# A state-space scan and a gated feed-forward on one core: block 0's scan as a pipeline over all PSUM banks, masked copies of C on ScalarE, the float64 conversion in two stages over three engines

## The chip, the core and the metric

The kernel runs on one core of a Trainium2 chip. A core has five engines that run their own queues in order and wait for each other through semaphores: TensorE (PE, matrix multiplies; its weight loads are listed apart as PEld), VectorE (DVE), ScalarE (ACT), GpSimd (POOL) and SyncE (SP, which here only issues DMAs). SBUF is the working memory of 128 partitions; PSUM holds what TensorE writes, in 8 banks of 128 x 512 float32. GpSimd has no access to PSUM in this kernel. The metric is the device time of one execution in microseconds, the median of several runs.

## The reference

Four sequences of 768 positions with 8 heads go through a linear recurrence (a state of 16 x 32 for each head), the heads are put side by side to rows of 256, and those rows go through a feed-forward with a cosine gate. Cut to what is computed:

```python
log_a = np.log(np.clip(a, 1e-06, 1.0))
for c in range(nc):                       # a, B, C, x of one chunk of 32 positions
    cum = np.cumsum(la, axis=-1)
    L = np.exp(cum[:, :, :, None] - cum[:, :, None, :]) * causal
    M = np.einsum('bhin,bhjn->bhij', Cc, Bc) * L
    y[:, :, sl] = (np.einsum('bhij,bhjd->bhid', M, xc)
                   + np.einsum('bhin,bhnd->bhid', Cc, state) * np.exp(cum)[:, :, :, None])
    state = decay_full * state + np.sum(Bx, axis=2)
x = y.transpose(0, 2, 1, 3).reshape(B * S, H * D)      # 3072 x 256
h = x @ w_in                                           # 256 -> 2048
out = ((h * np.cos(h)) @ w_out).astype(np.float32)     # 2048 -> 256
```

Here x, a, B and C are float32, and `w_in` and `w_out` are float64: the kernel reads each weight as two 32-bit words and makes a float32 of them by arithmetic on the bits.

## The kernel before, in words

The sequence is cut into NC = 6 blocks of 128 positions. A block c has a scan for each of the four sequences ("batches", b) and a feed-forward over its 512 rows in NF = 16 steps f of 128 hidden columns.

The scan of one batch is written in four functions. `decays` makes `lam`, the decay matrix of all 8 heads, as a running product on VectorE (L231; in block 0 on PSUM tiles `a_ps` that TensorE fills with broadcast rows of `cut`, L242 and L244; in later blocks on rows `arow` that DMAs broadcast). `turn` transposes B, the decay-scaled C (`sc`) and C on TensorE (`tp`, L254), copies two of them to `bcT` on ScalarE (L256) and makes `cT`, four masked copies of C for the heads, on VectorE (L259). `intra` multiplies them (`g`, L270) and applies `lam` on VectorE (`m`, L273). `finish` multiplies with x (`y`, L286), copies the result to `yT` on ScalarE (L291), and makes the next state (`s_ps` on TensorE L295, `state` on VectorE L299, in later blocks two GpSimd operations). `prep` scales B and C of a block on GpSimd (`sc`, L220) with `dec`, the exponentials of summed logarithms that TensorE and ScalarE make at the start (L197 to L208).

A feed-forward step is `first` (two multiplies into `hp`, L314; `w` and `k` on ScalarE in block 0, `turns` on VectorE), `gate` one step later (`cos` on ScalarE, `gT` on VectorE) and `second` three steps later (four multiplies into `o`, L340). `hp` has three PSUM banks, so `hp` of step n needs `gT` of step n − 3. The scan's tiles, `a_ps` among them, share three more banks (tag "scan"), and `o` has the last two.

The weights come in 16 pieces of 128 x 512 elements, 8 of `w_in` and 8 of `w_out`, each good for two steps. `convert` takes one piece: ScalarE shifts the low word (`part`, L141), VectorE does four operations on the high word (`mag`: mask the sign L144, limit L146, shift L148, merge with sign and exponent L150), GpSimd adds the two (L154). The order of all work is written by hand: the program text is each engine's order. In it block 0's scan comes first, with three conversions ahead of it, batch after batch with `turn`, `intra`, `finish` in a row; then the 16 steps of block 0, each with one more conversion and a third of a batch of block 1's scan; then the same for later blocks without conversions. SP issues all loads but the first three pieces in the order of the text.

## Time and profile before

| | |
|---|---|
| median of 3 runs | 477.78 us (477.05 to 479.7) |
| the profiled execution, its own time | 476.28 us |
| its span on the core | 474.6 us |
| TensorE busy | 430.6 us (91%) |
| VectorE, ScalarE, GpSimd busy | 308.2, 153.6, 65.5 us |
| chain that ended last | PE 83%, DVE 13% of the span |

The page gives busy time of an engine over the whole span, a strip of 40 slices with the clock that the throttle granted to TensorE, the chain of work that ended last, and groups of instructions by line. A timeline gives single rows in order of time: start, length, engine, line, operation, tile written and tiles read, shape, count, and in brackets how long the engine had been idle and what ended that. A table of stretches gives each engine's busy time in a stretch, the granted clock and the DMA share. The end of a TensorE row is modelled, and rows of float32 matrix multiplies come two for one instruction.

### The profile page before, as it was taken

How to read it: one execution, taken by the hardware profiler on the slowest of the kernel's cores; microseconds unless marked ns; L12 is line 12 of the kernel's file. 1: busy time of each engine (PE TensorE's matmuls, PEld its weight loads, DVE VectorE, ACT ScalarE, POOL GpSimd, SP SyncE). 2: the span in 40 equal slices, each digit the busy share in tenths (PEclk: the TensorE clock that was granted, in tenths of full speed). 3: DMA queues.
4: the chain of work that ended last, by engine and by line, in shares of the span. 5: the costliest groups of instructions: out<-in, count | busy, mean ns of one | idle time of the engine just before them, and what ended most of it. 6: DMA issues, size and time to landing. Idle time of an engine off the chain costs nothing.

```text
span 474.6 us, 5058 instructions
## 1 busy us (share of the span) xinstructions
PE 430.6 (91%) x1896; PEld 274.5 (58%) x1896; DVE 308.2 (65%) x468; ACT 153.6 (32%) x285; POOL 65.5 (14%) x72
## 2 busy tenths in 40 slices
PE   5067757988999999999999999999999999999996
PEld 5044324644666666666666666666666656666665
DVE  3834599777666677657666758666667767455452
ACT  4000254523543223234232323332333322342331
POOL 2310054342250101120111020111200000000000
PEclk9657879988999999999999999999999999999999
DMA  9998049511091111371111752001101000010001
GB/s 184 274 148 251 0 134 141 81 44 46 2 133 45 44 46 44 60 74 45 46 45 46 84 50 88 27 19 44 46 0 44 1 1 1 0 46 0 0 1 46
DMA packets 102873, 28.84 MB, mean 61 GB/s; under 512 B 74816, under 2 KB 98752, under 8 KB 102848
## 3 DMA queue, kind: packets, MB, share of 16 engines
q1 hardware_dynamic: 102032, 26.94, 30.2%
q10 hardware_dynamic: 816, 1.57, 1.0%
q8 instruction: 15, 0.25, 0.2%
q14 instruction: 10, 0.08, 0.1%
HBM read 25.26 MB, written 3.24 MB: 60 GB/s over the span
## 4 chain that ended last, share of the span: by engine, by line
PE 83%; DVE 13%; issue 2%; ACT 1%; POOL 1%; POOLq 0%; ACTq 0%
PE hp L314 34%; PE o L340 32%; PE g L270 6%; PE y L286 3%; PE s_ps L295 3%; DVE lam L244 2%; PE y L282 2%; DVE mag L146 2%; DVE lam L231 2%; DVE mag L144 1%; PE tp L254 1%; DVE mag L148 1%; DVE cT L259 1%; PE a_ps L242 1%; DVE turns L325 1%
## 5 line engine op out<-in xcount | busy, mean ns | idle before, releaser
L314 PE MATMUL hp<-yT,w_in 128*128 128x512 f32 x384 | 189.9, 619 | 5.8 <-DVE gT L332 5.8
L340 PEld LDWEIGHTS o<-w_out,gT 128*128 128x128 f32 x768 | 146.4, 191 | 61.1 <-issue 46.1
L340 PE MATMUL o<-w_out,gT 128*128 128x256 f32 x768 | 180.9, 379 | 0.0
L318 ACT ACTIVATE w<-hp 128x512 f32<-128x512 f32 x96 | 57.4, 598 | 218.6 <-PE hp L314 218.6
L314 PEld LDWEIGHTS hp<-yT,w_in 128*128 128x128 f32 x384 | 71.8, 197 | 75.3 <-issue 66.0
L323 DVE TENSOR_SCALAR k<-w 128x512 f32<-128x512 f32 x80 | 36.6, 457 | 99.9 <-ACT w L318 99.9
L325 DVE SCALAR_TENSOR_TENSOR turns<-k,w 128x512 f32<-128x512 f32 x96 | 68.6, 715 | 16.6 <-ACT k L321 13.8
L332 DVE TENSOR_TENSOR gT<-hp,cos 128x512 f32<-128x512 f32 x96 | 65.6, 683 | 0.2 <-ACT cos L330 0.2
L330 ACT ACTIVATE cos<-turns 128x512 f32<-128x512 f32 x96 | 59.8, 622 | 2.5 <-DVE turns L325 2.5
L231 DVE TENSOR_TENSOR_SCAN lam<-arow,unit 128x1024 f32<-128x1024 f32 x20 | 45.6, 2281 | 0.0
L270 PE MATMUL g<-cT,bcT 64*128 64x512 f32 x96 | 29.2, 686 | 13.2 <-DVE cT L259 13.1
L305 POOL TENSOR_TENSOR state<-state,old 128x256 f32<-128x256 f32 x16 | 12.3, 766 | 186.7 <-DVE state L299 186.5
L273 DVE TENSOR_TENSOR m<-g,lam 128x512 f32<-128x512 f32 x48 | 30.7, 682 | 6.5 <-PE g L270 6.5
L291 ACT COPY yT<-y 128x256 f32<-128x256 f32 x24 | 9.0, 373 | 46.8 <-PE y L286 46.8
L299 DVE TENSOR_TENSOR state<-s_ps,own 128x256 f32<-128x256 f32 x20 | 8.5, 424 | 20.3 <-PE s_ps L295 20.3
L154 POOL TENSOR_TENSOR w_in<-mag,part 128x512 uint32<-128x512 uint32 x8 | 12.7, 1593 | 56.5 <-DVE mag L150 54.5
L286 PE MATMUL y<-m,xr 128*32 128x128 f32 x384 | 17.3, 294 | 3.4 <-DVE m L273 3.4
L270 PEld LDWEIGHTS g<-cT,bcT 64*128 64x128 f32 x96 | 7.4, 189 | 21.3 <-DVE cT L259 21.3
L154 POOL TENSOR_TENSOR w_out<-mag,part 128x512 uint32<-128x512 uint32 x8 | 14.5, 1809 | 33.8 <-DVE mag L150 31.7
L259 DVE TENSOR_TENSOR cT<-tp,slot 128x512 f32<-128x512 f32 x24 | 16.0, 668 | 4.0 <-ACT bcT L256 4.0
L256 ACT COPY bcT<-tp 128x256 f32<-128x256 f32 x24 | 8.9, 370 | 29.2 <-PE tp L254 29.2
L254 PE MATMUL tp<-ident,sc 128*128 128x128 f32 x24 | 6.7, 281 | 12.1 <-POOL sc L220 12.1
(52 smaller groups left out, 214.5 us busy)
## 6 DMA issues: line engine op xcount, KB each, us to landing
arow<-a_cut SPq DMA_DIRECT2D x20, 512.0 KB, 3.8
words<-in_moe_w_out_dram SPq DMA_DIRECT2D x8, 512.0 KB, 3.7
xr<-in_x_dram SPq DMA_DIRECT2D x6, 512.0 KB, 8.6
out_dram<-ob SPq DMA_DIRECT2D x12, 256.0 KB, 2.3
words<-in_moe_w_in_dram SPq DMA_DIRECT2D x5, 512.0 KB, 7.5
words<-in_moe_w_in_dram ACTq DMA_DIRECT2D x3, 512.0 KB, 6.5
bc<-in_B_dram SPq DMA_DIRECT2D x6, 256.0 KB, 6.6
bc<-in_C_dram SPq DMA_DIRECT2D x6, 256.0 KB, 9.1
```

The source lines that it names most:

```text
L154: G.tensor_tensor(out=dst.bitcast(U32), in0=bits.rearrange("p (k f) -> p k f", k=k), in1=part_.rearrange("p (k f) -> p k f", k=k), op=ALU.add)
L231: V.tensor_tensor_scan(out=l.rearrange("p h i -> p (h i)"), data0=arow.pop((c, b)).rearrange("p h i -> p (h i)"), data1=unit.rearrange("p ...
L270: PE.matmul(g[u], lhsT=bcT[r, 0], rhs=cT[r], start=True, stop=True)
L273: V.tensor_tensor(out=m[:, hs], in0=g[u], in1=l[:, hs], op=ALU.mult)
L286: PE.matmul(y[32 * q:32 * q + 32, t], lhsT=xr[:, b, h], rhs=m[:, h], start=(c == 0 and t == 0), stop=True, tile_position=(0, 32 * q), skip ...
L314: PE.matmul(hp[n], lhsT=w_in[:, k, f * P:(f + 1) * P], rhs=yT[c][:, k], start=(k == 0), stop=(k == KT - 1))
L318: ACT.activation(w, hp[n], AF.Copy, bias=0.25, scale=INV_2PI)
L323: V.tensor_scalar(out=k_, in0=w, scalar1=ROUND, scalar2=None, op0=ALU.add)
L325: V.scalar_tensor_tensor(out=turns[n], in0=k_, scalar=ROUND, in1=w, op0=ALU.subtract, op1=ALU.subtract)
L330: ACT.activation(cos, turns.pop(n), AF.Sin, scale=-TWO_PI)
L332: V.tensor_tensor(out=gT[n], in0=hp.pop(n), in1=cos, op=ALU.mult)
L340: PE.matmul(o[c][b // 2][:, b % 2], lhsT=g[:, b * P:(b + 1) * P], rhs=w_out[:, f], start=(f == 0 and b % 2 == 0), stop=(f == NF - 1), skip ...
```

## The change

Block 0's scan is written as a pipeline. `a_ps` is made by `spread_a`, ahead of everything on TensorE, for three of the four batches into banks of all three tags ("h" and "o" aren't in use yet), for the fourth when the first two banks are free. The logarithm's path moves into `whole`, behind them. `cut` is limited by GpSimd itself instead of being a copy of VectorE's result. `turn` for batch b + 1 or b + 2 stands ahead of `intra` for b, block 0 doesn't make the scaled C any more (its first state is zero), and the states of block 0 are made in `carry` after all four batches. `cT` is made by four ScalarE copies with a scale per partition, in all blocks; VectorE's operation goes. Conversion is split: `grade` (ScalarE takes the absolute value and shifts the low word, GpSimd limits) and `join` one step later (VectorE shifts and merges, GpSimd adds); one conversion stands ahead of block 0's batches and one behind them, instead of three ahead and two behind. The pieces are fetched and converted in the order in which the steps use them. `k`, `turns` and `cos` share one buffer in place, with four of them.

The diff, cut to its core:

```diff
-    def bank(shape, name):
-        return psum.tile(shape, FP32, tag="scan", bufs=3, name=name)
+    BANKS = {"scan": 3, "h": 3, "o": 2}
+    def bank(shape, name, tag="scan"):
+        return psum.tile(shape, FP32, tag=tag, bufs=BANKS[tag], name=name)
...
-    def convert(which, i):
+    held = {}
+    def grade(which, i):
...
-        part_ = conv.tile([P, 2 * WC], U32, tag="part", name="part")
-        ACT.activation(part_, low, AF.Copy, scale=2.0 ** -29)
-        mag = conv.tile([P, 2 * WC], FP32, tag="mag", name="mag")
-        bits = mag.bitcast(U32)
-        V.tensor_scalar(out=bits, in0=high, scalar1=0x7FFFFFFF, scalar2=None,
-                        op0=ALU.bitwise_and)
-        V.tensor_scalar(out=mag, in0=mag, scalar1=LEAST, scalar2=MOST,
-                        op0=ALU.max, op1=ALU.min)
+        mag = conv.tile([P, 2 * WC], FP32, tag="mag", bufs=3, name="mag")
+        ACT.activation(mag, high.bitcast(FP32), AF.Abs)
+        last = conv.tile([P, 2 * WC], U32, tag="last", bufs=3, name="last")
+        ACT.activation(last, low, AF.Copy, scale=2.0 ** -29)
+        G.tensor_scalar(out=mag, in0=mag, scalar1=MOST, scalar2=LEAST,
+                        op0=ALU.min, op1=ALU.max)
+        held[which, i] = (high, mag.bitcast(U32), last)
+    def join(which, i):
+        if (which, i) not in held:
+            return
+        high, bits, last = held.pop((which, i))
         V.tensor_scalar(out=bits, in0=bits, scalar1=3, scalar2=0x3FFFFFFF,
                         op0=ALU.logical_shift_left, op1=ALU.bitwise_and)
...
         G.tensor_tensor(out=dst.bitcast(U32), in0=bits.rearrange("p (k f) -> p k f", k=k),
-                        in1=part_.rearrange("p (k f) -> p k f", k=k), op=ALU.add)
-    for i in range(3):
-        fetch("in", i, nc.scalar)
+                        in1=last.rearrange("p (k f) -> p k f", k=k), op=ALU.add)
+    order = [(w, i) for i in range(NPC) for w in ("in", "out")]
+    for n in (0, 2, 1):
+        fetch(*order[n], nc.scalar)
     load(0)
-    for i in range(3, 6):
-        fetch("in", i)
-        if i < 5:
-            fetch("out", i - 3)
+    for n in range(3, 8):
+        fetch(*order[n])
...
-    G.tensor_copy(out=cut, in_=la)
+    G.tensor_scalar(out=cut, in0=a_in, scalar1=1.0, scalar2=1e-6, op0=ALU.min, op1=ALU.max)
...
+    def spread_a(b, tags):
+        u, b_ = b // (NB // NU), b % (NB // NU)
+        spread[b] = []
+        for t in range(2):
+            a_ps = bank([P, HH, P], "a_ps", tags[t])
+            for h in range(HH):
+                r = (b_ * H + t * HH + h) * NC
+                PE.matmul(a_ps[:, h], lhsT=ident[0:RB, r:r + 1].to_broadcast([RB, P]),
+                          rhs=cut[:, u], start=(h == 0), stop=True, skip_group_check=True)
+            spread[b].append(a_ps)
...
-        cT = scan.tile([P, HH, P], FP32, tag="cT", name="cT")
-        V.tensor_tensor(out=cT, in0=tp[:, 2].unsqueeze(1).to_broadcast([P, HH, P]),
-                        in1=slot.unsqueeze(2).to_broadcast([P, HH, P]), op=ALU.mult)
+        cT = scan.tile([P, HH, P], FP32, tag="cT", name="cT")
+        for t in range(HH):
+            ACT.activation(cT[:, t], tp[:, 1], AF.Copy, scale=slot[:, t:t + 1])
...
-        g = [bank([P, HH, P], "g") for _ in range(2)]
+        g = [bank([P, HH, P], "g", "scan" if c > 0 else "h") for _ in range(2)]
...
-        y = bank([P, 2, P], "y")
+        y = bank([P, 2, P], "y", "scan" if c > 0 else "o")
...
-        turns[n] = ffn.tile([P, TB], FP32, tag="turns", name="turns")
-        V.scalar_tensor_tensor(out=turns[n], in0=k_, scalar=ROUND, in1=w,
+        turns[n] = k_
+        V.scalar_tensor_tensor(out=k_, in0=k_, scalar=ROUND, in1=w,
                                op0=ALU.subtract, op1=ALU.subtract)
...
     load(1)
+    load_a(1)
+    for n in range(8, len(order)):
+        fetch(*order[n])
+    load(2)
+    spread_a(0, ("h", "h"))
+    spread_a(1, ("h", "o"))
+    spread_a(2, ("o", "scan"))
+    grade("in", 0)
     decays(0, 0)
     decays(0, 1)
-    load_a(1)
-    for i in range(3):
-        convert("in", i)
+    whole()
+    spread_a(3, ("h", "h"))
     prep(0)
+    turn(0, 0)
+    turn(0, 1)
+    decays(0, 2)
+    join("in", 0)
+    intra(0, 0)
+    finish(0, 0)
+    decays(0, 3)
+    turn(0, 2)
+    intra(0, 1)
+    finish(0, 1)
+    turn(0, 3)
+    intra(0, 2)
+    finish(0, 2)
+    intra(0, 3)
+    finish(0, 3)
+    grade(*order[1])
+    grade(*order[2])
+    join(*order[1])
     for b in range(NB):
-        turn(0, b)
-        intra(0, b)
-        finish(0, b)
-        if b + 2 < NB:
-            decays(0, b + 2)
...
+        carry(0, b)
     prep(1)
...
             first(n)
+        if c == 0 and n + 3 < len(order):
+            grade(*order[n + 3])
...
-        if c == 0:
-            if f % 2 == 0 and 4 + f // 2 < NPC:
-                convert("in", 4 + f // 2)
-            if f % 2 == 1 and 1 + f // 2 < NPC:
-                convert("out", 1 + f // 2)
+        if c == 0 and n + 2 < len(order):
+            join(*order[n + 2])
```

What that makes of three queues follows, in the order in which instructions stand (no time is in it). First TensorE from its first matrix multiply on, before:

```order
L200 MATMUL lt_ps<-ident,la 128x96 x2
L207 MATMUL d_ps<-laT,upto 128x192
L207 MATMUL d_ps<-laT,after 128x192
L207 MATMUL d_ps<-laT,ones 128x192
L242 MATMUL a_ps<-cut,ident 128x128 x16
L254 MATMUL tp<-ident,bc 128x128
L254 MATMUL tp<-ident,sc 128x128
L254 MATMUL tp<-ident,bc 128x128
L270 MATMUL g<-cT,bcT 128x512 x2
L286 MATMUL y<-m,xr 32x128 x8
```

And now:

```order
L252 MATMUL a_ps<-cut,ident 128x128 x24
L214 MATMUL lt_ps<-ident,la 128x96 x2
L219 MATMUL d_ps<-laT,upto 128x192
L219 MATMUL d_ps<-laT,after 128x192
L219 MATMUL d_ps<-laT,ones 128x192
L252 MATMUL a_ps<-cut,ident 128x128 x8
L276 MATMUL tp<-ident,bc 128x128
L277 MATMUL tp<-ident,bc 128x128
L276 MATMUL tp<-ident,bc 128x128
L277 MATMUL tp<-ident,bc 128x128
L298 MATMUL g<-cT,bcT 128x512 x2
L314 MATMUL y<-m,xr 32x128 x8
```

The broadcasts of three batches moved ahead of the logarithm's transposes and sums, and the transposes read B and C alone, with a second batch's ahead of the first `g`.

Next VectorE, from the first running product to the first feed-forward update (`k` written in place), now. Before, three conversions of four operations each stood between the first `lam` rows and the first `cT`, two more behind block 0's last state.

```order
L267 SCALAR_TENSOR_TENSOR lam<-a_ps,unit 128x512 x6
L158 TENSOR_SCALAR mag<-mag 128x512
L160 SCALAR_TENSOR_TENSOR mag<-words,mag 128x512
L301 TENSOR_TENSOR m<-g,lam 128x512 x2
L267 SCALAR_TENSOR_TENSOR lam<-a_ps,unit 128x512 x2
L301 TENSOR_TENSOR m<-g,lam 128x512 x6
L158 TENSOR_SCALAR mag<-mag 128x512
L160 SCALAR_TENSOR_TENSOR mag<-words,mag 128x512
L332 TENSOR_TENSOR state<-s_ps,own 128x256 x4
L358 SCALAR_TENSOR_TENSOR k<-k,w 128x512
L158 TENSOR_SCALAR mag<-mag 128x512
L160 SCALAR_TENSOR_TENSOR mag<-words,mag 128x512
```

The last batch's `lam` now stands between the first and the second batch's `m`, the join of the second piece between the last `m` and the four states, and the join of the third piece behind the first update of the feed-forward.

Last ScalarE, in one feed-forward step of block 0 in which a batch of block 1 is turned, before (from one `cos` to the next):

```order
L330 ACTIVATE cos<-turns 128x512
L141 ACTIVATE part<-words 128x512
L256 COPY bcT<-tp 128x256
L318 ACTIVATE w<-hp 128x512
L321 ACTIVATE k<-w 128x512
L330 ACTIVATE cos<-turns 128x512
```

And now (the row that writes and reads `k` is the cosine in place; `mag` is the absolute value and `last` the low word's shift):

```order
L363 ACTIVATE k<-k 128x512
L283 ACTIVATE cT<-tp,slot 128x128 x4
L286 COPY bcT<-tp 128x256
L351 ACTIVATE w<-hp 128x512
L354 ACTIVATE k<-w 128x512
L144 ACTIVATE mag<-words 128x512
L146 ACTIVATE last<-words 128x512
L363 ACTIVATE k<-k 128x512
```

Four masked copies stand between a `cos` and the next `w`, and two conversion operations, one more than before, now stand between `k` and `cos` instead of behind `cos`.

73 lines of the change are left out of this document (37 added, 36 removed).

## The prediction

> **What bounds the kernel now.** The table of stretches, cut where the feed-forward half of each block begins, comes first. Its columns are the stretch and its length, then busy time (and instructions) of TensorE, weight loads, VectorE, ScalarE and GpSimd, then granted clock and DMA.
>
> ```profile
> 0.00:55.61 55.61, 28.79 (x173) 19.10 (x174) 27.73 (x41) 9.63 (x19) 8.93 (x17) 0.77 0.93 183
> 55.61:139.64 84.03, 70.95 (x285) 41.72 (x284) 66.88 (x103) 38.23 (x69) 33.94 (x25) 0.89 0.47 79
> 139.64:207.67 68.03, 68.03 (x309) 43.59 (x308) 45.76 (x69) 21.70 (x42) 7.67 (x11) 1.00 0.27 53
> ```
>
> From 139.64 us TensorE is busy all the time at full clock: 68.03 us a block, and nothing on another engine shortens it. Ahead of that lie 55.61 us in which it idles half the time (block 0's scan) and block 0's feed-forward, 84.03 us long. Only these two stretches can shrink. What a feed-forward step costs when TensorE alone sets it is the distance between two `hp` groups with no scan between them, from the timeline:
>
> ```profile
> 143.09 1.88 PE L314 MATMUL hp<-yT,w_in 128*128 128x512 f32 x4
> 146.53 1.88 PE L314 MATMUL hp<-yT,w_in 128*128 128x512 f32 x4
> ```
>
> That is 3.44 us, so 16 steps are 55.0 and the next block's scan adds 68.03 − 55.0 = 13.0 us of TensorE work. The timeline of block 0 shows why the start is slow (start, length, engine, line, and in brackets the idle time before and its releaser):
>
> ```profile
> 4.50 0.10 POOL L195 MEMSET cut<- 96x2 f32 x1
> 7.08 1.78 ACT L208 ACTIVATE dec<-d_ps 128x192 f32<-128x192 f32 x3 [0.89 <-PE d_ps L207]
> 8.12 4.44 PE L242 MATMUL a_ps<-cut,ident 96*128 96x128 f32 x32
> 9.91 4.57 DVE L244 TENSOR_TENSOR_SCAN lam<-a_ps,unit 128x512 f32<-128x512 f32 x4 [3.99 <-PE a_ps L242]
> 21.60 0.69 DVE L150 SCALAR_TENSOR_TENSOR mag<-words,mag 128x512 uint32<-128x512 uint32 x1
> 24.77 0.48 PE L254 MATMUL tp<-ident,sc 128*128 128x128 f32 x1 [12.10 <-POOL sc L220]
> 26.64 2.08 PE L270 MATMUL g<-cT,bcT 64*128 64x512 f32 x4 [1.19 <-DVE cT L259]
> ...
> 50.35 0.37 ACT L256 COPY bcT<-tp 128x256 f32<-128x256 f32 x1 [0.61 <-PE tp L254]
> 50.76 0.69 DVE L259 TENSOR_TENSOR cT<-tp,slot 128x512 f32<-128x512 f32 x1 [0.36 <-ACT bcT L256]
> 51.50 1.13 PE L270 MATMUL g<-cT,bcT 64*128 64x512 f32 x4 [1.24 <-DVE cT L259]
> 52.66 1.29 DVE L273 TENSOR_TENSOR m<-g,lam 128x512 f32<-128x512 f32 x2 [1.21 <-PE g L270]
> 54.01 0.66 PE L286 MATMUL y<-m,xr 128*32 128x128 f32 x8 [0.17 <-DVE m L273]
> 54.73 0.37 ACT L291 COPY yT<-y 128x256 f32<-128x256 f32 x1 [4.00 <-PE y L286]
> 55.61 4.91 PE L314 MATMUL hp<-yT,w_in 128*128 128x512 f32 x9
> 55.85 0.42 DVE L299 TENSOR_TENSOR state<-s_ps,own 128x256 f32<-128x256 f32 x1 [1.90 <-PE s_ps L295]
> ```
>
> Three weight pieces are converted on VectorE up to 21.60, GpSimd scales C behind them, and TensorE waits 12.10 us for that. Then each batch walks transposes, copies, `g`, `m`, `y` one after another.
>
> **Part 1: up to the first g.** The broadcast `a_ps` no longer stands behind `lt_ps` and `d_ps`, so TensorE starts it when `cut` is ready, about 4.4. A bank at half clock takes 9.91 − 8.12 = 1.79 us; the other three in the 4.44 us took (4.44 − 1.79)/3 = 0.88, at full clock. When does the clock rise?
>
> ```profile
> 35.00:36.00 1.00, 0.00 (x0) 0.00 (x0) 1.00 (x2) 0.24 (x1) 0.00 (x0) 1.00 1.00 284
> 36.62 1.86 PE L270 MATMUL g<-cT,bcT 64*128 64x512 f32 x4 [1.79 <-DVE cT L259]
> 37.00:38.00 1.00, 1.00 (x4) 0.00 (x0) 0.00 (x0) 0.00 (x0) 0.00 (x0) 0.50 1.17 290
> 54.00:55.00 1.00, 0.99 (x9) 0.61 (x10) 0.00 (x0) 0.27 (x2) 0.00 (x0) 0.50 0.00 0
> 57.00:58.00 1.00, 1.00 (x3) 0.41 (x2) 0.93 (x3) 0.00 (x0) 0.00 (x0) 0.82 0.00 0
> ```
>
> Some 3.3 us after dense work begins at 54 (clock 0.50) it is back (0.82 in 57 to 58). So six banks end at about 4.4 + 2 × 1.75 + 4 × 0.88 = 11.4. Six scans of 4.57/4 = 1.14 us end at 13.6. The logarithm's transposes and sums follow the banks; table load and three `dec` (1.78/3 = 0.6 each) on ScalarE give the first `dec` at 14.0. The third `d_ps` takes the bank of scan six, 14.0, then two banks for batch 3 (1.8) and the transposes: 16.1. C must have landed:
>
> ```profile
> L92 SPq DMA_DIRECT2D bc<-in_C_dram x1: 7087/7087/7087, 1.7 to 1.7; - x1
> DMA to landing us min/median/max: 12.2/12.2/12.2
> ```
>
> 1.75 + 12.2 = 13.95, in time. The four masked copies on ScalarE replace one 0.69 on VectorE. The trace has no 128x128 copy with a scale from memory; the nearest is `bcT`, 0.37 for twice the width. I take 0.3 each (0.2 to 0.5), 1.5 with `bcT`: first `g` at 17.6, against 26.64 before.
>
> **Part 2: the four batches.** Batch 0's two `g` halves share one bank, since batch 3's `a_ps` holds the other two: 0.95 + 0.64 + 0.95 + 0.64, `y` 0.5, to 21.4. Batch 3's two scans (2.3) stand on VectorE between m(0) and m(1), so m(1) runs 23.2 to 24.5, `y` to 25.0. The last two cost what the rows from 51.50 to 54.67 show, 3.2 each, as transposes and copies are already done: 31.5, `yT` 31.9. Batches at half clock cost about 1 us more each (0 to 4 in all); I add 2: **33.9**.
>
> [...]
>
> **Part 3: into the feed-forward.** The fourth `s_ps` needs a bank freed by state 0, and on VectorE the join of the second weight piece now stands ahead of the states. That join waits for ScalarE (Abs, behind the last `yT`) and GpSimd's clamp. So a new wait: Abs 0.6, clamp 0.75, shift 0.45, merge 0.69, state 0.42, and `s_ps`, shorter than a `g`, 0.6: 3.6 with hand-overs, where 0.5 lay between 55.1 and 55.61. The clamp has no row; `cut` and the adds bound it, 0.39 for half the width and 1.30 for two inputs:
>
> ```profile
> 4.04 0.39 POOL L194 COPY cut<-la 96x256 f32<-96x256 f32 x1 [0.57 <-DVE la L192]
> 14.83 0.43 DVE L146 TENSOR_SCALAR mag<-mag 128x512 f32<-128x512 f32 x1
> 16.59 1.30 POOL L154 TENSOR_TENSOR w_in<-mag,part 128x512 uint32<-128x512 uint32 x1 [12.00 <-DVE mag L150]
> 16.81 1.37 DVE L146 TENSOR_SCALAR mag<-mag 128x512 f32<-128x512 f32 x1
> ```
>
> First `hp` at **37.5**, 18.1 earlier.
>
> ```profile
> 58.40 0.60 ACT L318 ACTIVATE w<-hp 128x512 f32<-128x512 f32 x1 [2.18 <-PE hp L314]
> 59.03 0.63 ACT L321 ACTIVATE k<-w 128x512 f32<-128x512 f32 x1
> 61.60 1.28 ACT L330 ACT_TABLE_LOAD   x1
> 67.57 3.68 PE L314 MATMUL hp<-yT,w_in 128*128 128x512 f32 x4 [5.77 <-DVE gT L332]
> ```
>
> hp(0) cold 3.0, hp(1) 1.7: 42.2. hp(2) needs the second piece of w_in, joined on VectorE after the first `k` update: 40.5 + w and k 1.3 + update 0.7 + shift and merge 1.1 + add 1.3 + hand-overs, 45.2. That is another new wait, 3 us, and hp(2) is cold, 3.4. hp(3) at 48.6; its `gT` (two more ACTIVATEs on ScalarE ahead of the table load) is ready by 48. So 11.1 us from hp(0) to hp(3), 12.0 before (67.57 − 55.61).
>
> **Part 4: the rest of block 0.** 13 steps and block 1's scan are 13 × 3.44 + 13.0 = 57.7 us of TensorE work; before they took 139.64 − 67.57 = 72.1, 14.4 more. The rows of one batch:
>
> ```profile
> 77.22 2.29 DVE L231 TENSOR_TENSOR_SCAN lam<-arow,unit 128x1024 f32<-128x1024 f32 x1
> 80.00 1.11 DVE L325 SCALAR_TENSOR_TENSOR turns<-k,w 128x512 f32<-128x512 f32 x1
> 80.14 1.13 PE L270 MATMUL g<-cT,bcT 64*128 64x512 f32 x4 [3.39 <-DVE cT L259]
> 81.20 3.68 PE L314 MATMUL hp<-yT,w_in 128*128 128x512 f32 x4
> ```
>
> `g` waited for `cT`, which stood behind the 2.29 us scan, and the next `hp` ran at half clock (3.68 for 1.88): some 5 us a batch, in three batches. With `cT` on ScalarE that goes. What is late next: VectorE still has, for three steps, 3 × (k update 0.6 + `gT` 0.6 + join 1.1, as they follow each other) + scan 2.2 + `m` 1.3 + state 0.4 = 10.8 us, while TensorE needs 3 × 3.44 + 13.0/4 = 13.6. So it fits, but its shift shares with GpSimd: 0.43 alone and 1.37 beside an add. GpSimd gets a clamp a step more. And `hp` of every even step waits for its piece: from the `hp` two steps earlier it is 1.9 to its end, 3.7 for five ACTIVATEs up to `gT`'s end with it, 1.1 for the join and 1.3 for the add, some 8.2 with hand-overs, where TensorE is free after 6.9 and whatever scan matmuls lie between (0.3 to 2.7). So some stall, others don't. I keep 7 us of the 14.4 (0 to 14.4). Block 1 starts at 48.6 + 57.7 + 7 = 113.3, 26.3 earlier.
>
> **Part 5: blocks 1 to 5.** Nothing. All waits before `g` sum to
>
> ```profile
> L270 PE MATMUL g<-cT,bcT 64*128 64x512 f32 x96 | 29.2, 686 | 13.2 <-DVE cT L259 13.1
> ```
>
> and lie before 139.64, as TensorE is 68.03 of 68.03 busy after. The masked copies add 4 × 1.2 us a block to ScalarE's 21.70 of 68.03, hidden by TensorE. The in-place k, `turns`, `cos` cost nothing for the same reason.
>
> **Sum.** Span 474.6 − 26.3 = 448.3; with the 1.7 us around it 450.0, against 476.28 for the profiled execution. The median of the runs shown is 1.5 above that one, so 451.
>
> **Rivals.**
> 1. *Full clock, few stalls*: block 0 stays warm (−2), hp(0) and hp(2) nearly (−3), the rest loses 2 instead of 7: 441. For it: the `g` at 51.50 took 1.13 (2.08 at 26.64), though TensorE had idled 1.24 just before. [...] Chance 0.2.
> 2. *The conversion stays the bound*: clamps, adds, shifts and k updates get in each other's way, all 14.4 or a little more stay, 459 to 463. For it: the 1.37 and 1.11 rows. [...] Chance 0.2.
> 3. *Slower*: the masked copies. They stand on ScalarE between `cos` and the next `w`. From transposes to the end of that `hp` some 2 us are free, and hp's third bank gives about 3 more; past 1.1 us a copy TensorE stalls in every batch. At 1.7 us a copy, 2.3 us × 20 batches, about 497. Against it: 0.37 for twice the width. Chance 0.05.
> 4. *It doesn't do what it says*: the start is set by transfers, not by the order, and block 0 ends where it did, 475 to 478. Against it: C landed at 13.95, 10.8 before TensorE used it. Chance 0.03.
>
> The forecast itself, 444 to 457, has 0.52. The range 439 to 463 takes in rivals 1 and 2. Faster by over 0.5% (what a measurement of this kernel can tell from no change) 0.92, within 0.03, slower 0.05.
>
> **What would show it.** First `g` near 17.6 and first `hp` near 37.5; three us of idle before the third `hp` group, released by GpSimd's add; no wait of `g` for VectorE; the second stretch about 76 long; blocks of 68.0 from then on. It is wrong if blocks 1 to 4 change length, if a masked copy takes over 0.5, if the clamp takes over 1.3, or if block 1 starts after 125.

## The result and the profile after

The changed kernel takes **451.08 us** (median of 4 runs, 449.82 to 455.56) where the kernel before takes 477.41 beside it: a ratio of 0.946, 95% interval 0.938 to 0.954. The forecast was 451, but the profiled execution shows the sum coming out by other terms than written. It took 455.56 us with a span of 453.8, the longest of the four; two other runs had spans of 448.1 and 448.2, where 448.3 was forecast. In the second set of runs below one, of 454.82 us, counts as slow and stays out of the ratio.

The table of stretches of the changed kernel, cut at the first `hp` of block 0, at that of block 1 and one block later. Columns as in the prediction: busy time of TensorE, weight loads, VectorE, ScalarE and GpSimd, then granted clock and DMA.

```profile
0.00:41.79 41.79, 29.44 (x168) 17.92 (x169) 19.87 (x28) 14.54 (x37) 8.10 (x18) 0.84 1.06 208
41.79:119.08 77.29, 68.69 (x286) 40.79 (x285) 54.31 (x76) 49.32 (x98) 46.51 (x40) 0.93 0.57 104
119.08:187.11 68.03, 68.03 (x310) 43.59 (x309) 43.99 (x66) 25.81 (x58) 7.60 (x11) 1.00 0.29 55
```

Of the 20.6 us by which block 1 starts earlier (119.08 for 139.64), 13.8 lie ahead of the first `hp` and 6.7 in the stretch behind it; a block is 68.03 us as before. The timeline of block 0's scan:

```profile
4.87 8.88 PE L252 MATMUL a_ps<-cut,ident 96*128 96x128 f32 x48 [4.87 <-POOL cut L205]
12.00 3.45 DVE L267 TENSOR_TENSOR_SCAN lam<-a_ps,unit 128x512 f32<-128x512 f32 x3 [0.38 <-PE a_ps L252]
18.14 1.15 ACT L283 ACTIVATE cT<-tp,slot 128x128 f32<-128x128 f32 x4 [1.37 <-PE tp L277]
19.50 1.12 PE L298 MATMUL g<-cT,bcT 64*128 64x512 f32 x2 [1.17 <-ACT bcT L288]
24.93 2.19 PE L298 MATMUL g<-cT,bcT 64*128 64x512 f32 x4
27.04 1.29 DVE L301 TENSOR_TENSOR m<-g,lam 128x512 f32<-128x512 f32 x2 [1.00 <-PE g L298]
31.70 1.29 DVE L301 TENSOR_TENSOR m<-g,lam 128x512 f32<-128x512 f32 x2 [3.37 <-PE g L298]
35.74 1.29 DVE L301 TENSOR_TENSOR m<-g,lam 128x512 f32<-128x512 f32 x2 [2.75 <-PE g L298]
```

The scans show the pace of the spread `a`: they start at 6.99, 8.69, 10.40 and 12.00, so four banks took 1.7 us each and the last two 1.0. The first `g` comes at 19.50 and the batches follow each other 4.0 to 4.7 us apart (the `m` rows), each `g` of 2.1 to 2.2 us being at half clock (1.13 at full). Then the way into the feed-forward half and its first groups:

```profile
37.58 0.37 ACT L319 COPY yT<-y 128x256 f32<-128x256 f32 x1 [3.44 <-PE y L314]
37.85 0.67 ACT L144 ACTIVATE mag<-words 128x512 f32<-128x512 f32 x1
38.61 0.61 POOL L147 TENSOR_SCALAR mag<-mag 128x512 f32<-128x512 f32 x1 [19.80 <-ACT mag L144]
39.26 0.43 DVE L158 TENSOR_SCALAR mag<-mag 128x512 uint32<-128x512 uint32 x1 [2.23 <-POOL mag L147]
39.72 1.15 DVE L160 SCALAR_TENSOR_TENSOR mag<-words,mag 128x512 uint32<-128x512 uint32 x1
40.79 1.63 DVE L332 TENSOR_TENSOR state<-s_ps,own 128x256 f32<-128x256 f32 x4
41.26 0.70 PE L328 MATMUL s_ps<-xr,sc 128*128 128x256 f32 x2 [2.25 <-DVE state L332]
41.79 5.29 PE L347 MATMUL hp<-yT,w_in 128*128 128x512 f32 x8
49.54 5.25 PE L347 MATMUL hp<-yT,w_in 128*128 128x512 f32 x8 [2.46 <-POOL w_in L164]
59.60 3.62 PE L347 MATMUL hp<-yT,w_in 128*128 128x512 f32 x4 [2.76 <-POOL w_in L164]
```

Read down the chain, each step starts about where the one before it ends: Abs, clamp, shift, merge, state, the fourth `s_ps`, `hp`. That chain is the new wait forecast at 3.6 us; it took 3.84 from the last `yT`'s end (37.95). The third `hp` group waits 2.46 us for GpSimd's add, as forecast; the fifth does so again. The costliest groups:

```profile
L347 PE MATMUL hp<-yT,w_in 128*128 128x512 f32 x384 | 187.7, 613 | 8.2 <-POOL w_in L164 8.2
L283 ACT ACTIVATE cT<-tp,slot 128x128 f32<-128x128 f32 x96 | 27.4, 367 | 16.0 <-PE tp L279 14.1
L298 PE MATMUL g<-cT,bcT 64*128 64x512 f32 x96 | 31.6, 707 | 2.0 <-ACT bcT L288 1.2
```

Before `g` 2.0 us of idle are left of 13.2, none of it for a `cT`: 1.2 us are for `bcT` at the first `g`, and 0.79 for the first `m` on VectorE, since the two halves of batch 0's `g` share a bank (21.40). A masked copy takes 0.367 us on average, and four in a row 1.15, as they overlap.

**Where the clock changes.** Block 0's scan ran at half clock for 13.7 us. The trace's first change of the clock is at 21.98 and its last ahead of block 1 at 62.94, twelve times 3.413 us apart. Cut at multiples of 3.413 us from 21.98, every row of the changed kernel has one clock:

```profile
18.57:21.98 3.41, 1.70 (x4) 0.59 (x4) 0.69 (x1) 2.08 (x9) 0.24 (x1) 1.00 1.05 379
21.98:25.39 3.41, 3.21 (x22) 1.15 (x22) 2.37 (x3) 0.66 (x3) 0.00 (x0) 0.50 1.31 268
...
32.22:35.63 3.41, 3.18 (x20) 0.91 (x20) 0.77 (x2) 0.37 (x1) 0.00 (x0) 0.50 1.29 179
...
39.05:42.46 3.41, 1.20 (x4) 0.87 (x5) 3.00 (x6) 1.14 (x3) 2.29 (x4) 1.00 1.12 304
42.46:45.87 3.41, 3.41 (x5) 1.35 (x4) 0.00 (x0) 1.04 (x2) 1.80 (x2) 0.50 0.59 205
```

The second number after the window is TensorE's busy time. A window at full clock with 1.70 or 1.20 us of work is followed by one at half; a window at half clock followed by one at full is almost full here, but not every such window is (3.18 of 3.41 was enough at 32.22, 3.21 at 21.98 was not). In the trace of the kernel before, all changes of the clock, from 16.45 to 118.84 us, lie on a grid of the same spacing (102.39 us, thirty times 3.413). Two of its rows on that grid:

```profile
33.52:36.93 3.41, 1.62 (x14) 1.37 (x15) 2.92 (x3) 0.37 (x1) 0.00 (x0) 0.99 1.06 273
36.93:40.34 3.41, 2.64 (x20) 0.40 (x16) 1.29 (x2) 0.00 (x0) 0.00 (x0) 0.50 1.20 289
```

In both traces the clock fell behind a row with about half its length of work (1.70 and 1.62 us). The prediction has no grid: of this place in before it shows only single rows, a gap of 1.79 us up to 36.62 and half clock from 37.

### The profile page after: what moved, and what is told of

It is laid out like the page before. It is cut to its first block, busy times and chain, and to the rows that moved or that the text cites. A ratio compares the mean times of both kernels' runs of the same rounds, so it can differ in the third digit from the quotient of the medians.

```text
span 453.8 us, 5045 instructions
## 1 busy us (share of the span) xinstructions
PE 428.9 (95%) x1892; PEld 272.4 (60%) x1892; DVE 279.8 (62%) x411; ACT 186.0 (41%) x398; POOL 78.0 (17%) x87
## 4 chain that ended last, share of the span: by engine, by line
PE 85%; DVE 6%; ACT 3%; issue 2%; DMA 2%; POOL 2%
PE hp L347 35%; PE o L373 33%; PE g L298 6%; PE y L314 3%; PE s_ps L328 2%; PE a_ps L252 2%; PE y L310 2%; DVE mag L160 1%; POOL w_in L164 1%; DVE m L301 1%; DMA arow<-a_cut 1%; DVE lam L260 1%; DMA a_in<-in_a_dram 1%; DVE mag L158 1%; ACT mag L144 1%
## 5 line engine op out<-in xcount | busy, mean ns | idle before, releaser
L358 DVE SCALAR_TENSOR_TENSOR k<-k,w 128x512 f32<-128x512 f32 x96 | 72.6, 756 | 16.1 <-ACT k L354 13.3
L365 DVE TENSOR_TENSOR gT<-hp,k 128x512 f32<-128x512 f32 x96 | 65.7, 684 | 8.5 <-ACT k L363 8.5
L363 ACT ACTIVATE k<-k 128x512 f32<-128x512 f32 x96 | 59.7, 622 | 0.8 <-DVE k L358 0.8
L301 DVE TENSOR_TENSOR m<-g,lam 128x512 f32<-128x512 f32 x48 | 31.0, 686 | 17.2 <-PE g L298 17.2
L283 ACT ACTIVATE cT<-tp,slot 128x128 f32<-128x128 f32 x96 | 27.4, 367 | 16.0 <-PE tp L279 14.1
L298 PE MATMUL g<-cT,bcT 64*128 64x512 f32 x96 | 31.6, 707 | 2.0 <-ACT bcT L288 1.2
L314 PEld LDWEIGHTS y<-m,xr 128*32 128x32 f32 x384 | 9.0, 112 | 13.2 <-DVE m L301 9.7
L147 POOL TENSOR_SCALAR mag<-mag 128x512 f32<-128x512 f32 x16 | 12.1, 754 | 26.7 <-ACT mag L144 26.7
L164 POOL TENSOR_TENSOR w_in<-mag,last 128x512 uint32<-128x512 uint32 x8 | 14.4, 1794 | 11.9 <-DVE mag L160 11.9
L164 POOL TENSOR_TENSOR w_out<-mag,last 128x512 uint32<-128x512 uint32 x8 | 14.0, 1750 | 12.7 <-DVE mag L160 12.7
L328 PE MATMUL s_ps<-xr,sc 128*128 128x256 f32 x40 | 13.4, 426 | 2.3 <-DVE state L332 2.3
```

Of the source, the lines that this page charges most:

```text
L164: G.tensor_tensor(out=dst.bitcast(U32), in0=bits.rearrange("p (k f) -> p k f", k=k), in1=last.rearrange("p (k f) -> p k f", k=k), op=ALU.add)
L298: PE.matmul(g[u], lhsT=bcT[r, 0], rhs=cT[r], start=True, stop=True)
L301: V.tensor_tensor(out=m[:, hs], in0=g[u], in1=l[:, hs], op=ALU.mult)
L314: PE.matmul(y[32 * q:32 * q + 32, t], lhsT=xr[:, b, h], rhs=m[:, h], start=(c == 0 and t == 0), stop=True, tile_position=(0, 32 * q), skip ...
L358: V.scalar_tensor_tensor(out=k_, in0=k_, scalar=ROUND, in1=w, op0=ALU.subtract, op1=ALU.subtract)
L363: ACT.activation(cos, cos, AF.Sin, scale=-TWO_PI)
```

## The experiments

In the figures below, "stretch" is the time from block 0's first `hp` to block 1's, by each trace's timeline, or, where block 1's start is hidden in a merged row, by its span less the 334.7 us of blocks 1 to 5. Times are medians; the kernel before beside them is at 477.1 to 477.5. Two medians stand for the changed kernel, 451.08 and 449.61.

### The changed kernel again

No edit.

> The changed kernel once more, unaltered, to see how far its profiled execution depends on where the granted clock changes. In the first trace every edge of the granted clock from 21.98 to 62.93 us (0.50 or back to 1.00) lies on a grid of 3.413 us, and so do all edges of the kernel before (16.45 to 118.84). Theory (the clock is decided once per grid window from how busy TensorE was in it): the edges lie again on such a grid, at another phase; block 0's scan has more or fewer windows at half clock than the four of the first trace, the first hp moves with it between 37.5 and 43, and the span between 446 and 455; blocks 1 to 5 stay at 334.7 +- 0.5. Rival (the 5.5 us that the first trace lies above the forecast come from waits): first hp again at 41.5 to 42.1 and the span 453 to 454.5, whatever the edges.

449.61 us (447.73 to 454.82), ratio 0.941 (0.938 to 0.944). The profiled execution has the span 448.1, first `hp` at 38.45, block 1 at 113.39. Its windows, cut on a grid from 20.07:

```profile
16.66:20.07 3.41, 1.99 (x10) 0.92 (x9) 0.22 (x1) 2.49 (x10) 1.18 (x1) 0.99 1.02 362
20.07:23.48 3.41, 2.68 (x14) 0.73 (x14) 1.21 (x3) 0.00 (x0) 0.00 (x0) 0.50 1.04 377
23.48:26.90 3.42, 3.37 (x14) 1.08 (x14) 2.42 (x3) 1.67 (x6) 0.00 (x0) 0.51 0.99 109
26.90:30.31 3.41, 2.28 (x22) 0.82 (x22) 1.47 (x3) 1.67 (x6) 0.00 (x0) 1.00 1.02 104
40.55:43.96 3.41, 1.49 (x4) 0.38 (x2) 2.05 (x4) 3.35 (x7) 1.77 (x3) 1.00 0.97 342
43.96:47.37 3.41, 1.98 (x4) 0.68 (x4) 2.04 (x2) 3.19 (x5) 2.12 (x2) 1.00 0.43 155
```

Two windows at half clock in the scan instead of four, and the one after the first `hp` gone: here the grid falls so that the dense piece from 23.5 fills a window (3.37 us of 3.42), and the next is at full clock. The same program, 5.7 us shorter. The theory holds, for these two traces; of the other runs only the spans are known. The lower edge is not sharp, though: a window with 1.99 lowered the clock, those with 1.49 and 1.98 didn't.

### Masked copies of C back on VectorE

The four copies go, and one multiply stands behind `bcT`:

```
-            ACT.activation(cT[:, t], tp[:, 1], AF.Copy, scale=slot[:, t:t + 1])
+        V.tensor_tensor(out=cT, in0=tp[:, 1]..., in1=slot..., op=ALU.mult)
```

> The changed kernel with the masked copies of C back on VectorE as one multiply behind bcT; all else as changed. Theory A (g no longer standing behind the lam scan is worth about 6 us): g waits again for cT in the second stretch, over 6 us summed, the stretch from first hp to block 1 grows from 77.3 to 82-87 us; block 0's scan is about 1 us shorter (0.69 for 1.15 a batch); time 5 us above the changed kernel (2 to 9), some 456. Theory B (VectorE's relief by the two-stage conversion is what ended those waits, and the copies could stay): g's waits under 3 us, the stretch 76-79, time within 1.5 us of the changed kernel or up to 2 faster.

460.98 us (458.02 to 462.21), ratio 0.964 (0.961 to 0.967): 10 to 11 above the changed kernel, more than the 2 to 9 expected. The stretch is 82.1 us. The group of `g`, and the timeline at one of its waits and in the scan:

```profile
L298 PE MATMUL g<-cT,bcT 64*128 64x512 f32 x96 | 32.9, 731 | 10.5 <-DVE cT L287 7.1 <-DVE m L301 3.4
18.36 1.12 PE L298 MATMUL g<-cT,bcT 64*128 64x512 f32 x2 [0.86 <-DVE cT L287]
22.84 2.07 PE L298 MATMUL g<-cT,bcT 64*128 64x512 f32 x2 [3.37 <-DVE m L301]
114.38 1.68 PE L298 MATMUL g<-cT,bcT 64*128 64x512 f32 x4 [2.08 <-DVE cT L287]
```

Three waits of 2.1 us behind the `lam` scan are back, two of them with a half-clock window behind (97.8, 114.9). The 3.37 us were not foreseen: in this trace batch 2's scans (2.33 us from 18.82) and the first join (from 21.06), which the changed kernel runs while TensorE spreads `a`, stood in VectorE's order behind a `cT` that waits for the transposes (17.61), and the `m` behind them came at 22.11. Theory A holds, and the copies are worth more than the scan behind which `g` stood.

### The conversion in one stage

The steps taken out stand in `grade`, those put in in `join`:

```
-        ACT.activation(mag, high.bitcast(FP32), AF.Abs)
-        G.tensor_scalar(out=mag, ..., op0=ALU.min, op1=ALU.max)
+        V.tensor_scalar(out=bits, in0=high, scalar1=0x7FFFFFFF, ..., op0=ALU.bitwise_and)
+        V.tensor_scalar(out=mag, ..., op0=ALU.max, op1=ALU.min)
```

> The changed kernel with the sign mask and the clamp of a weight piece back on VectorE, in join (four VectorE steps a piece, no Abs on ScalarE, no clamp on GpSimd); all else as changed. Theory B (two stages are worth several us): VectorE's busy time between first hp and block 1 rises from 54.3 by 13 x 0.86 = 11 to about 65 us of 77, the stretch grows by 4 (2 to 8) us, the wait of hp for w_in from 8.2 to 11 or more, time some 455. Theory A (only the masked copies matter): the stretch stays at 77 +- 1.5 and the time within 1.5 us of the changed kernel; the way from the last y to the first hp gets shorter by some 0.5 us, as Abs and the clamp's hand-over drop out.

457.16 us (454.95 to 459.9), ratio 0.958 (0.955 to 0.962): 6 to 7.5 above the changed kernel. The stretch, and `hp`'s waits:

```profile
36.86:118.47 81.61, 68.97 (x285) 40.55 (x284) 68.11 (x104) 42.52 (x85) 37.51 (x27) 0.94 0.62 115
L349 PE MATMUL hp<-yT,w_in 128*128 128x512 f32 x384 | 187.4, 612 | 10.5 <-POOL w_in L166 10.5
```

VectorE carries 68.11 us where the changed kernel has 54.31, and the stretch is 4.3 us longer (6.7 longer than the 74.94 of the second trace). The two stages also cost something: from the last `yT` to the first `hp` this kernel takes 1.99 us (34.87 to 36.86), the changed one 3.84 and 3.38, for there the join waits for Abs and clamp. Theory B holds too: both parts are needed, neither makes up for the other.

### The clamp alone on VectorE

Out of `grade`, into `join`:

```
-        G.tensor_scalar(out=mag, ..., op0=ALU.min, op1=ALU.max)
+        V.tensor_scalar(out=mag, ..., op0=ALU.min, op1=ALU.max)
```

> The changed kernel with the clamp of a weight piece on VectorE, ahead of join's shift, instead of on GpSimd; Abs stays on ScalarE. Theory (GpSimd's clamp costs little, 0.61 us beside other work; VectorE's step of 0.43 lengthens each join): VectorE's busy time from first hp to block 1 rises by 13 x 0.45 = 6 us, hp's waits for w_in grow by 1 to 3 us in sum; time 2 us above the changed kernel (0 to 4), some 451.5. Rival (VectorE and GpSimd holding each other off is the price of the two-stage form, the clamp's 0.6 to 1.05 us a piece above all): fewer stretched steps, time 1 to 4 us below the changed kernel.

452.59 us (450.99 to 456.06), ratio 0.949 (0.946 to 0.953): 1.5 to 3 above. `hp` waits 9.7 us for w_in in all instead of 8.2, VectorE is busy 60.79 us in the stretch. GpSimd's clamp earns its place, by little.

### The kernel before with masked copies only

```
-        V.tensor_tensor(out=cT, in0=tp[:, 2]..., in1=slot..., op=ALU.mult)
+        for t in range(HH):
+            ACT.activation(cT[:, t], tp[:, 2], AF.Copy, scale=slot[:, t:t + 1])
```

> The kernel before with nothing changed but the multiply of C by slot: four masked copies on ScalarE, behind bcT, in its place. With the copies taken out of the changed kernel its time rose by 11.4 us, so theory A now has them worth 6 to 11 us in the kernel before too: the stretch from first hp to block 1 falls from 84.0 to 74-79 us, g's waits fall from 13.2 to under 6 us, block 0's scan grows by about 2 us (four copies in a row for one multiply, four times); time 471 (467 to 475). Rival (the copies only pay together with the lighter conversion, since the 2.2 us scans then meet four VectorE steps a piece): the stretch stays above 81, the time within 2 us of before, 476 to 480.

469.21 us (467.85 to 473.0), ratio 0.985 (0.981 to 0.988): 8 below the kernel before. The stretch falls from 84.0 to 78.4 us. `g`'s waits are 6.1 us instead of 13.2, all in block 0's scan, where each `cT` now takes four copies behind `bcT`; the scan got no longer all the same (first `hp` at 54.23 for 55.61). With one wait gone, another shows, four groups into the feed-forward half:

```profile
66.21 3.78 PE L314 MATMUL hp<-yT,w_in 128*128 128x512 f32 x4 [6.11 <-DVE gT L332]
```

### The kernel before with two conversions moved

The second loop stands behind block 0's scan:

```
-    for i in range(3):
-        convert("in", i)
+    convert("in", 0)
     prep(0)
...
+    for i in range(1, 4):
+        convert("in", i)
     convert("out", 0)
```

> The kernel before with two of the three conversions at the start (pieces 1 and 2 of w_in) moved behind block 0's scan; no new banks, no pipeline over batches, no masked copies. Theory (of the 13.8 to 17 us by which the first hp came earlier, the moved conversions alone are half): first g at 19 to 21 instead of 26.64, first hp at 47 to 50 instead of 55.61; then the conversions stand between the last y and hp(2), as joins do in the changed kernel, and w_out's first piece comes 4 us later, so the stretch from first hp to block 1 grows by 2 to 5 us; time 473 (469 to 476). Rival (the banks and the pipeline are what moves the first hp): first hp at 53 to 56 and the time within 1.5 us of before, or above it.

476.26 us (473.88 to 480.27), ratio 1.000 (0.996 to 1.003): nothing, as the rival has it. The rows of this kernel at the first `g` and in the feed-forward half:

```profile
21.20 2.08 PE L270 MATMUL g<-cT,bcT 64*128 64x512 f32 x4 [1.19 <-DVE cT L259]
...
52.84 6.26 PE L314 MATMUL hp<-yT,w_in 128*128 128x512 f32 x12
70.67 3.78 PE L314 MATMUL hp<-yT,w_in 128*128 128x512 f32 x4 [11.56 <-DVE gT L332]
```

The first `g` comes 5.4 us earlier, the first `hp` 2.8, and the conversions then stand ahead of the gate: 11.56 us. The expectation, 4 us faster, missed that `gT(0)` and not `w_in` would be late. A conversion of four VectorE steps is paid once, ahead of the scan or behind it. The move accounts for 2.8 of the 13.8 to 17.2 us by which the changed kernel's first `hp` is earlier (41.79 and 38.45 for 55.61); the rest is put down to the pipeline over banks and batches, which was not tried alone.

### The joins earlier

The second and third piece are graded and joined in block 0's scan or right behind the states, and each later one a step earlier (`grade(*order[n + 4])`, `join(*order[n + 3])`):

```
     turn(0, 3)
+    grade(*order[1])
     intra(0, 2)
     finish(0, 2)
+    join(*order[1])
+    grade(*order[2])
     intra(0, 3)
     finish(0, 3)
-    grade(*order[1])
-    grade(*order[2])
-    join(*order[1])
     for b in range(NB):
         carry(0, b)
+    join(*order[2])
+    grade(*order[3])
```

> The changed kernel with the second and third weight pieces graded and joined inside block 0's scan or right behind the states, and every later grade and join one step earlier; nothing else. Theory (the joins ahead of the states and of hp(2), hp(4) are new waits, each followed by a window at half clock): last y to first hp 2 us instead of 3.8; no wait of hp for w_in at the third and fifth group (2.46 and 2.76 before); the stretch from first hp to block 1 falls from 77.3 to 68-72; time 9 us below the changed kernel (5 to 13), some 441. Rival (other waits stand right behind: pieces that have not landed, gT, ScalarE's chain): hp waits as long for another releaser, time within 3 us of the changed kernel.

445.16 us (443.5 to 448.89), ratio 0.933 (0.929 to 0.936): 4.5 to 6 below the changed kernel, not 9. No `hp` waits for w_in any more and the stretch is 70.2 us, but from the last `yT` to the first `hp` it takes 2.95 us (at half clock), not 2, and the fourth group has a new wait. ScalarE and TensorE there:

```profile
46.90 0.65 ACT L146 ACTIVATE last<-words 128x512 uint32<-128x512 uint32 x1
47.57 1.28 ACT L363 ACT_TABLE_LOAD   x1
48.87 0.63 ACT L363 ACTIVATE k<-k 128x512 f32<-128x512 f32 x1
...
50.27 3.01 PE L347 MATMUL hp<-yT,w_in 128*128 128x512 f32 x4 [3.98 <-DVE gT L365]
```

The Sin of step 0 (`k<-k`) stands behind a grade and the load of its table. Both readings were half right: the joins were the waits, and another stood 4 us behind. This run's scan was also at half clock throughout (six windows, 20.4 to 40.9).

### The gate ahead of the grade, the table loaded early

On top of the earlier joins:

```
     whole()
+    ACT.activation(early, ones[:, 0:1], AF.Sin)
...
+        if 0 <= n - 1 < NC * NF:
+            gate(n - 1)
         if c == 0 and n + 4 < len(order):
             grade(*order[n + 4])
-        if 0 <= n - 1 < NC * NF:
-            gate(n - 1)
```

> The kernel with the joins early, and two things more: Sin's table is loaded during block 0's scan, by a Sin of one column behind the three dec, and in block 0's steps the gate of step n-1 stands ahead of the grade of step n+4 on ScalarE. With the joins early alone, hp(3) waited 3.98 us for gT(0), whose Sin stood behind two grades (2 x 1.3) and a table load (1.28), and a window at half clock followed. Theory (that wait is the rest of the gain): hp(3) waits under 1.8 us for gT, no table load behind first hp, no window at half clock behind hp(3); time 3 us below joins-early (1.5 to 5), some 442. Rival (the next link is VectorE's k update, held beside GpSimd's adds, or the one load merely moves into the scan's chain): hp(3) still waits over 3 us or first g comes 1 us later, time within 1 us of joins-early.

442.43 us (440.66 to 444.23), ratio 0.928 (0.924 to 0.931), as expected in time; yet `hp(3)` still waits 3.26 us for `gT(0)`, not under 1.8, and a window at half clock (49.0 to 52.4) follows again. The rival named the next link: VectorE's steps ahead of `gT(0)`, slowed beside GpSimd (the rows of the next kernel show them).

### g of the next batch ahead of y

On top of that, and alike for the batches behind:

```
     intra(0, 0)
-    finish(0, 0)
     decays(0, 3)
     turn(0, 2)
     intra(0, 1)
-    finish(0, 1)
+    finish(0, 0)
...
```

> The same as gate-first, with each batch's g put ahead of the y of the batch before it in block 0's scan, so that TensorE has work while VectorE multiplies m, and its windows are fuller. Theory (in block 0's scan TensorE's waits for m, 0.7 to 1.0 us a batch, are chain time and also keep the clock at half): last yT 2 us earlier than in gate-first at the same clock, fewer windows at half clock; time 2 us below gate-first (0 to 4), some 440. Rival (three banks for g: the second half of a g waits for m of the batch before, so nothing overlaps): waits of g for m take the place of y's, time within 1 us of gate-first.

**440.33 us** (439.54 to 441.17), ratio 0.923 (0.920 to 0.926), as expected; the first `hp` is at 34.90 (39.02 with the gate first). In the traces TensorE's waits ahead of `y` fall from 2.6 to 0.9 us, those ahead of `g` rise from 2.0 to 2.5, and two windows of the scan are at half clock instead of four, at another place of the grid; what the order gave in waits and what in clock was not separated. Its runs lie within 1.6 us, those of the changed kernel within 7. The wait of `hp(3)`, and VectorE beside GpSimd ahead of it:

```profile
38.55 2.69 POOL L235 TENSOR_TENSOR sc<-bc,dec 128x512 f32<-128x512 f32 x2
39.06 1.28 DVE L158 TENSOR_SCALAR mag<-mag 128x512 uint32<-128x512 uint32 x1
40.37 1.43 DVE L160 SCALAR_TENSOR_TENSOR mag<-words,mag 128x512 uint32<-128x512 uint32 x1
43.47 3.48 PE L347 MATMUL hp<-yT,w_in 128*128 128x512 f32 x4 [3.26 <-DVE gT L365]
```

Behind the k update, shift and merge take 1.28 and 1.43 beside GpSimd's scalings, 0.43 and 0.69 alone.

### The scalings of block 1 earlier

On top of that, from behind the states into the scan:

```
     finish(0, 1)
+    prep(1)
     join(*order[1])
...
-    prep(1)
```

> The same as g-ahead, with GpSimd's two scalings of block 1's B and C (2.69 us behind first hp in that run) moved ahead, into the end of block 0's scan. In g-ahead three VectorE steps beside them took 1.03 (k update), 1.28 (shift) and 1.43 us (merge), where they take 0.69, 0.43 and 0.69 alone; gT(0) came behind them and hp(3) waited 3.26 us for it. Theory (VectorE held off while GpSimd runs is what hp(3) waits for): those steps back at 0.7, 0.45 and 0.7, hp(3) waits 1.7 us (1.0 to 2.2); time 1.6 us below g-ahead (1 to 3.4, more where the half-clock window behind hp(3) goes), some 438.5. Rival (ScalarE's row of six steps is the next link, or the scalings hold up m(3) in the scan instead): hp(3) still waits over 2.6 us or first hp comes 1 us later, time within 0.7 us of g-ahead.

440.49 us (439.11 to 440.57), ratio 0.923 (0.920 to 0.926): no different from the kernel with `g` ahead. The wait of `hp(3)` falls as the theory has it, to the expected 1.7, and is paid in the scan, as the rival has it: TensorE's waits ahead of `y` grow from 0.9 to 3.3 us, and the first `hp` comes at 37.48 instead of 34.90, in a trace with three windows at half clock in the scan instead of two.

```profile
32.60 1.43 DVE L160 SCALAR_TENSOR_TENSOR mag<-words,mag 128x512 uint32<-128x512 uint32 x1
34.78 0.93 PE L314 MATMUL y<-m,xr 128*32 128x128 f32 x16 [1.69 <-DVE m L301]
44.46 1.99 PE L347 MATMUL hp<-yT,w_in 128*128 128x512 f32 x4 [1.67 <-DVE gT L365]
```

### Filling TensorE's gaps, twice

Products that nobody reads. In the changed kernel, eight behind the second batch's transposes and four behind each `g`, into the `tp` bank; then, in the kernel with the gate first, two behind each `g`, into the `y` bank:

```
+    for _ in range(8):
+        PE.matmul(part_tp[1][:, 2], lhsT=ident, rhs=ident, start=True, stop=True)
...
+            for _ in range(2):
+                PE.matmul(y0[b][:, 0], lhsT=ident, rhs=ident, start=True, stop=True, ...)
```

> The changed kernel with products that nobody reads, put where TensorE waits in block 0's scan: eight 128x128 behind the second batch's transposes and four behind each batch's g, into the third part of the tp banks. Theory (a grid window of 3.413 us in which TensorE is busy over about half keeps the full clock, and at half clock one busy for over some 3.2 us gives it back): at most two windows of block 0's scan at half clock, in most runs one or none, where the two traces of the changed kernel have four and two; first hp at 37 to 39; time 2 us below the changed kernel (0.5 to 4), and its runs lie closer together. Rival (the clock follows something else than how busy TensorE is, so fill only delays): as many windows at half clock, first hp 0.3 to 1.5 us later, time 0 to 2 us above the changed kernel.

> The same as gate-first, with two 128x128 products that nobody reads behind each batch's g in block 0's scan, written to the y bank ahead of y (no wait for ScalarE), 0.55 us at full clock by the 8 records in 1.16 us of the first fill, and 1.0 at half. Theory (fuller windows give the full clock back): runs lie closer together and the median is 1 us below gate-first (-0.5 to 3), as one or two windows fewer run at half. Rival (fill costs what it gains: at half clock it is longer than the gap of 0.8): 0 to 1.5 us above gate-first.

The first takes 453.25 us (452.48 to 454.54), ratio 0.950 (0.948 to 0.953), 2 to 3.6 above the changed kernel: wrong in time, right in that its runs lie closer together (2.1 us apart). In its trace three windows of the scan are at half clock (21.9 to 32.2), not at most two, and the first `hp` comes at 44.57, not at 37 to 39. The first fill there:

```profile
20.46 2.47 PE L412 MATMUL tp<-ident 128*128 128x128 f32 x16 [2.37 <-ACT bcT L291]
```

It waited 2.37 us for ScalarE to be done with the bank that it writes, and then took 2.47 us for eight products. The trace has two records for each, 16 in all; transposes, with one record, start 0.11 us apart. The first `g` began at 22.86 instead of 19.50. The second takes 442.64 us (438.46 to 443.36), ratio 0.927 (0.922 to 0.931), the same as without it (442.43), and its runs lie further apart (4.9 us for 3.6), not closer. Two of its six runs, the profiled one among them (span 436.8), had no change of the clock ahead of the first `hp`:

```profile
18.71:22.12 3.41, 2.63 (x24) 1.14 (x22) 1.67 (x3) 0.48 (x3) 0.00 (x0) 1.00 1.04 385
22.12:25.54 3.42, 3.31 (x30) 1.60 (x26) 3.23 (x4) 1.67 (x6) 0.00 (x0) 1.00 0.93 105
```

Of the other that is read from its mean clock, 0.994 in both; the remaining four stood at 0.984 to 0.988. So fuller windows go with full clock here (2.24 to 3.41 us of work in each from 15.30 to 39.19), but this fill had that in two runs of six, and in the median it earns nothing.

## Why the prediction was right, point by point

- **Blocks 1 to 5: nothing.** Right: 334.7 us from 119.08 to the span's end, 335.0 before. The masked copies there are hidden behind TensorE.
- **Part 1, first g at 17.6.** Late by 1.9 in the profiled execution (19.50), by 1.1 in the second trace of the same kernel (18.69). `cut` came at 4.8, not 4.4, and four banks instead of two ran at half speed: 8.88 us for six, taken as 7.0. Four copies and `bcT` were sized 1.5 and took 1.15 + 0.28.
- **Part 2, last yT at 33.9.** Here the sum failed most: 37.95, and 35.07 in the second trace. From the first `g` on that is 18.5 us and 16.4, for 16.3 in the sum. The step "Batches at half clock cost about 1 us more each (0 to 4 in all); I add 2" allowed for half the batches. In the profiled execution the four batches, with gaps of 0.7 to 0.8 us, left 2.75 to 3.21 us of work in each window of the grid from 21.98 to 35.63, and batches 1 to 3 ran at half. That VectorE's scans would hold m(1) to 23.2 was beside the point: m(1) waited for a `g` at half clock until 27.04.
- **Part 3, tail 3.6 and hp(0) to hp(3) in 11.1.** Tail 3.84, 11.1 measured (41.79 to some 52.9): right in this execution, with the clamp at 0.61 for 0.75 taken and the merge at 1.15 for 0.69, since it met GpSimd's next clamp. In the second trace the first groups were at full clock: 3.38 and 9.3.
- **Part 4, excess of 7 us over 57.7.** 8.5 in the profiled execution (119.08 − 52.9 − 57.7), 8.0 in the second trace (hp(3) there at 47.72). Right in size, near enough, and in cause: the joins of even steps, whose waits in this part sum to 5.75 us (2.76, 1.50, 1.49). That one of them is 2.76 long at the fifth group, with half clock behind it, and that adds of GpSimd last 3.2 us beside a `lam` scan (1.5 us late at 81.07 and 110.44) was foreseen only as "some stall".
- **The sum.** Block 1 at 113.3 forecast; 119.08 in the profiled execution, 113.39 in the second. The way there was as described, but that the figures meet so closely is luck. In the second trace errors cancel: the first `g` is 1.1 us late and part 4 is 1.0 longer, while hp(0) to hp(3) are 1.8 shorter. And the 1.5 us added for the median, from before, went the other way: here the median lies 4.5 us below the profiled execution, the longest of its four.
- **The rivals.** Full clock (441) did not come by itself; in the trace with the small fill, where it came, every window of the scan held 2.24 us of work or more, and how full windows are was not in the prediction. "The conversion stays the bound" is the kernel with one stage, 457, not the changed one. That steps of VectorE and GpSimd get in each other's way is borne out (in the changed kernel an add takes 1.3 us in most places and 3.2 beside a `lam` scan; a shift takes 0.43 there and 1.28 beside a scaling in the kernel with `g` ahead) and cost some 1.5 us at a time, not 14. The masked copies, by the prediction's estimate, needed 1.1 us each to hurt, and took 0.37.

What each part is worth, by the runs: masked copies 8.2 us alone (477.4 − 469.2) and 10 to 11 with the rest in place (461.0 − 451.1 or 449.6); two stages 6 to 7.5 with the rest in place. Of the 26 to 28 us that leaves, if the parts add up, some 9 to 12 to the pipeline over banks and batches with its moved conversions, which was not tried alone: that figure is a remainder, not a measurement, so what may be the largest share is argued rather than shown. Two conversions moved without the rest gave nothing.

## What to carry to other kernels

Where an in-order engine does both a long scan and a short step on another engine's path, move the short step; that was worth more here (10 to 11 us) than taking two of a conversion's four steps off the same engine (6 to 7.5). When a wait goes, look along the chain for the next before pricing the gain: joins, Sin's table, GpSimd's scalings each took the place of the last, and after three more edits the kernel stands at 440.3 us instead of 450. On TensorE, price a latency-bound stage, one in which it mostly waits, by how full its windows are, too, if its traces show a grid like the one of 3.413 us here; ordering real work so that it waits less and the windows fill gave 2 us, dummy work nothing in the median.

## What was not expected of the hardware

- In the traces of before, of the changed kernel and of the experiments, the changes of the granted clock lie on a grid of 3.413 us (thirty of it from 16.45 to 118.84 in before, twelve from 21.98 to 62.94 in the changed kernel). The grid's position differs between the two traces of the changed kernel (21.98 in one, 20.07 in the other), and with it the span: 453.8 and 448.1 us. All its runs lie between 446.0 and 453.8, but the others have no trace, and the mean clock doesn't order them strictly (450.5 us at 0.969, 453.8 at 0.972).
- How much work the windows held when the clock changed is not one number in these traces. At full clock, it fell behind every window with 1.47 us of TensorE work or less (1.47 at 45.65 of the kernel with the gate first; the rows ahead of a trace's first change are left aside) and behind none with over 2.2 (2.23 at 33.72 in the second trace of the changed kernel); between them both happened (2.19 at 19.45 of the kernel with the clamp on VectorE lowered it, 1.49 at 74.38 of the kernel with one stage did not). At half clock it never rose behind 2.98 us or less (2.98 at 27.22 of the kernel with the joins early); above that, it rose behind 2.99 us (39.74 in the kernel with the copies back on VectorE), behind 3.08 of `hp` alone (43.14 in the kernel with `g` ahead), and not behind 3.41 us of mostly `g` and `y` (22.66 there). Why was not tried by itself.
- Block 0's first products in the changed kernel, four banks of 1.7 us each from 4.87 where the next two took 1.0, ran at a little over half their later speed while the rows of that time say 1.00. The pace rises between 11.5 and 12.0, where the grid has an edge (21.98 − 3 × 3.413 = 11.74), so here the granted clock of the trace says nothing ahead of its first change.
